# Attention and a rational MLP on one core: the last 64 keys added to the sum tiles by accumulating transfers, and early weights parked every fourth pair

## The chip, the cores and the metric

One Trainium2 chip, one of its cores. The time is the device time of the kernel in microseconds; the median of three runs before is 660.2 us (659.58 to 661.03).

## What is computed

Softmax attention with a soft cap on the scores, for 4 batches of 12 heads with 448 positions and 64 channels, and behind it an MLP with a rational activation on the 1792 x 768 result. All data are float32.

```python
scores = scale * np.matmul(q, k.transpose(0, 1, 3, 2))        # scale = 1 / 8
scores = cap * np.tanh(scores / cap)
scores = scores - np.max(scores, axis=-1, keepdims=True)
attn = np.exp(scores)
attn = attn / (np.sum(attn, axis=-1, keepdims=True) + 1e-09)
x = np.matmul(attn, v)                                        # then (4*448, 12*64)
h = x @ w_in                                                  # 768 -> 2048
P = a[0] + a[1] * h + a[2] * h**2 + a[3] * h**3
Q = 1.0 + np.abs(b[0]) * np.abs(h) + np.abs(b[1]) * h**2
out = (P / (Q + 1e-6)) @ w_out                                # 2048 -> 768
```

The cap bounds the scores, so for a small enough cap the kernel leaves out the maximum (its "bounded" branch, the one that runs here) and puts a scaled guard in place of the 1e-9.

## The kernel before

**Pairs.** The attention stage works on 24 pairs of heads; `p` counts them, two pairs make a group of four heads that is loaded at once, `ring_of` names the buffer. For a pair, `prep_k` and `prep_q` transpose K and Q on TensorE (L343 to L366) and VectorE splits them into a high and a low part (L350 to L384). `scores` (L429) multiplies a tile of 128 keys by all queries of both heads, three products of high and low parts; a pair has three such tiles (n = 0, 1, 2). The 64 keys that are left over, the tail, are done for two pairs together as tile n = 3, in the odd pair: its rows 0 to 63 belong to the even pair, 64 to 127 to the odd one. `softmax` runs Tanh (L440) and Exp (L457) on ScalarE. `pv` (L511) multiplies by V for the three full tiles, `pv_tails` (L528) adds the tails of both pairs, and VectorE copies the results into the tiles U (L535).

**Sums.** VectorE adds the three exponential tiles of a pair to a sum tile `es[p % 6]` (L463, twice per pair); the tail is not in it. `norm4(k)` (L580) sums over the keys by matmuls with columns of ones (L594), for four pairs at once, into the bank `mi`: eight products of the sum tiles and four of the tails, each two instructions, 24 in all. VectorE copies the result (L598), four small transfers on POOL gather it, VectorE adds the guard and takes the reciprocal (L605, L606), one transfer writes it to DRAM (`dn`), and four broadcast it to all partitions (`bc`). `xout` (L627) multiplies U by it, `split_x` (L638, L639) splits the result for the MLP. `norm4` is called in pairs 5, 9, 13, 17 and 21, each time for the four pairs that began five pairs before; `norm` (L538) does two pairs, in pair 23 and at the end, with 16 instructions (L556).

**Order.** `visits(p)` writes the order of the steps of a pair by hand. In an even pair: s0 s1 s2, transposes of pair p + 2, `pv` and the tails of pair p - 1. In an odd one: s0 s1 s2, the scores of tile 3, the sum if it is due, the softmax of tile 3, the transposes of pair p + 2, `pv` of p - 1. All of TensorE's work in this stage writes the key "turn" and so keeps the written order. The other engines get their order from `Plan.flush`: it runs through all work once with assumed costs, and takes on each engine the ready piece with the lowest number, less its `early`. Each engine then executes that order as it stands; POOL and SP issue the transfers in it.

**Early weights.** The weights arrive as 64 bit words. `load_w` fetches a block of 768 KB, `make_w` builds float32 from it (ScalarE L789; VectorE L791, L794, L797) in a scratch tile XA, which lies over the tiles U of pairs 15 and 16. Four blocks are loaded in pairs 3, 5, 7 and 9 and built in the pair after. The first two are split at once into a high and a low part (L820, L822); the last two are parked: written to DRAM (`w32`) and read back by `unpark` later.

**MLP.** `stage1` multiplies x by a block of w_in, 36 matmuls per unit (units 0 to 3: L858, in turns of 512 and 384 columns; later ones: L843, all of 512 ahead of all of 384), `rational` (L889 to L902) the activation, `stage2` (L928) multiplies by w_out, and the evictions (L955, L961) collect the sums.

Of the kernel before, what the change touches and what calls it, by code (L numbers as in the profile page):

```python
# [16 lines left out]
ALU = mybir.AluOpType  # L17
# [7 lines left out]
NES = 6  # L25
# [22 lines left out]
FILL = (4, 4)  # L48
# [4 lines left out]
EARLY_STEP = 2  # L53
# [5 lines left out]
SC_NS = 615  # L59
TURN_NS = 200  # L60
SHAPE_NS = 130
PV_NS = 2220
TAIL_NS = 870
D_NS = 1430
D4_NS = 2210
# [7 lines left out]
class Plan:  # L73
# [7 lines left out]
    def __init__(self):  # L81
        self.ops = []
        self.wr, self.rd = {}, {}
        self.n = 0
        self.free = [4500.0, 4600.0, 3700.0, 3700.0, 9900.0]
        self.dma_free = 11000.0
        self.where, self.over = {}, {}
# [94 lines left out]
def ring_of(g):  # L182

    return g % 2 if g else 2
# [63 lines left out]
class Body:  # L248
# [11 lines left out]
    def __init__(self, tc, io, cst, bounded):  # L260
# [16 lines left out]
        self.plan = Plan()  # L277
        self.loaded = {(0, 0), ("v32", 0), ("v", 0)}
        self.units = [(g, m, y) for g in range(self.NG) for m in range(self.B // 2) for y in range(self.NCH)]
        self.wn = 0  # L280

# [50 lines left out]
    def prep_k(self, p):  # L332
# [16 lines left out]
        self.op(PE, 440 + SHAPE_NS, tk, self.raw_keys(p, "rk"), [bk, "turn"], early=E_TR)  # L349
# [4 lines left out]
    def prep_q(self, p):  # L354
# [19 lines left out]
        self.op(PE, 390, tq, self.raw_keys(p, "rq"), [bq, "turn"], early=E_TR)  # L374
# [26 lines left out]
    def fill(self, n):  # L401

        z = self.io["arena_r"][:, 0:512]
        for _ in range(n):
            self.op(PE, 213, lambda: self.nc.tensor.matmul(self.PS[0][:, 1], z[:, 0:128], z, start=True, stop=True),
                    [], [("ps", 0), ("psb", 0), "turn"])
# [8 lines left out]
    def scores(self, p, n):  # L415
# [15 lines left out]
        first = n == 0 or p % 2 and n == 2  # L431
        self.op(PE, SC_NS * len(sets) + TURN_NS * first, run, [k for name, _ in sets for k in K(name)], w, early=E_SC)

    def softmax(self, p, n):
# [6 lines left out]
        if self.bounded:  # L441
            self.exp(p, n, e, [ek], e, ek)

    def etile(self, p, n):
# [4 lines left out]
        return self.e[ie], ("e", ie)  # L449

    def exp(self, p, n, src, sk, e, ek):
# [11 lines left out]
        self.op(DVE, dve_ns(896), lambda: nc.vector.tensor_tensor(es, a, e, ALU.add), [ek] + [ak] * (n == 1), ks)  # L463
# [33 lines left out]
    def pv(self, p):  # L497
# [16 lines left out]

        self.op(PE, PV_NS + SHAPE_NS, run, [("rv", ring_of(g), 0)] + [t[1] for t in tiles], [pk, "turn"])

    def pv_tails(self, p):
# [14 lines left out]
        self.op(PE, TAIL_NS, run, [("v32", ring_of(g), 0), ("v32", ring_of(g), 1), ek], ["pv", "mi", "turn"])  # L532
# [5 lines left out]
    def norm(self, k):  # L538
# [10 lines left out]

        def sums():  # L550
            for last in range(2):
                for j in range(2):
                    for x in range(2):
                        h = 32 * (2 * j + x)
                        st, mv = (self.half[x], tail[:, j]) if last else (self.ones, es[x][:, j])
                        m = nc.tensor.matmul(D[h:h + 32], st, mv, start=not last, stop=last == 1)  # L556
            return m

        self.op(PE, D_NS + SHAPE_NS, sums, [("es", (2 * k + x) % NES) for x in range(2)] + [tk, "ones"], [dk, "turn"])
# [20 lines left out]
    def norm4(self, k):  # L580
# [4 lines left out]
        tails = [self.etile(2 * (k + y), 3) for y in range(2)]  # L585
        es = [("es", (2 * k + x) % NES) for x in range(4)]

        def sums():
            for last in range(3):
                for y in range(2):  # L590
                    for j in range(2):
                        h = 32 * (2 * y + j)
                        st, mv = (self.both, tails[y][0]) if last == 2 else (self.unit[last], self.es[es[2 * y + last][1]])
                        m = nc.tensor.matmul(D[h:h + 32], st, mv[:, j], start=not last, stop=last == 2)  # L594
            return m

        self.op(PE, D4_NS + SHAPE_NS, sums, [*es, *(t[1] for t in tails), "ones"], [dk, "turn"])
# [43 lines left out]
    def attention(self):  # L641
# [33 lines left out]
        def visits(p):  # L675
# [10 lines left out]
            if p == 0:  # L686
                return [s0, s1, (k, 1), (q, 1), s2, (self.fill, FILL[0])]
            if p == 1:
                return [s0, (self.fill, FILL[1]), s1, (k, 2), s2, t, (q, 2), (k, 3), (q, 3), (pv, 0)]
            if not p % 2:  # L690
                return [s0, s1, s2, *new, (pv, p - 1), (tails, p - 1)]
            sums = (norm, p // 2 - 1)
            if p == P1 - 1:
                return [s0, s1, (pv, p - 1), sums, s2, t]
            four = [(norm4, p // 2 - 2)] * (p % 4 == 1)
            return [s0, s1, s2, (self.scores, p, 3), *four, (self.softmax, p, 3), *new, (pv, p - 1)]
# [637 lines left out]
```

## Time and profile before

| | us |
|---|---|
| median of three runs | 660.2 (659.58 to 661.03) |
| the profiled execution, its own time | 659.91 |
| its span, from the first to the last instruction | 657.9 |
| TensorE matmul busy (share of the span) | 647.8 (98%) |
| VectorE busy | 541.9 (82%) |
| ScalarE busy | 442.2 (67%) |
| POOL busy | 85.0 (13%) |

A row of the timeline begins with the start and the duration in microseconds, then the engine, the line of the kernel, the operation, target and sources, the count; in brackets stands the idle time before it and what ended it. Matmuls overlap, so the distance of two starts tells what a block took. In the table by stretches each engine has its busy time and, in brackets, its instructions; the granted clock is a share of full speed, and the DMA share is the mean over the core's 16 DMA engines. The attention stage ends at some 186 us, where the tails and the last sum are done.

### The profile page before, as it was taken

The numbers are of one execution on the slowest core, as the hardware profiler recorded it, in microseconds if no ns is written. First come the engines' busy times: TensorE is split into PE (matmuls) and PEld (weight loads), VectorE is DVE, ScalarE is ACT, GpSimd is POOL, SyncE is SP. The second block draws the span as 40 slices with busy tenths as digits, with TensorE's granted clock in tenths as the row PEclk, the third lists the DMA queues.
The fourth block names the chain that finished last, engine by engine and source line by source line (L and its number), as shares of the span: only waits on it lengthen the run. The fifth ranks groups of instructions, "written<-read, shape, count | busy, mean of one in ns | idle before, by whom it ended". The sixth has DMA issues, their size and how long they took to land.

```text
span 657.9 us, 9767 instructions
## 1 busy us (share of the span) xinstructions
PE 647.8 (98%) x3820; PEld 542.0 (82%) x3820; DVE 541.9 (82%) x662; ACT 442.2 (67%) x531; POOL 85.0 (13%) x141
## 2 busy tenths in 40 slices
PE   8999999999999999999999999999999999999996
PEld 5555555655478899999999999999999999999996
DVE  4789899899679987977987897899699789969653
ACT  5899999999857867875457466646646565663560
POOL 4013222321200000020012002101200210120030
PEclk9999999999999999999999999999999999999999
DMA  7757864943230332195158118614821671481086
GB/s 170 186 138 171 203 163 100 199 119 85 59 86 22 128 141 92 51 197 113 48 106 158 49 49 152 158 43 86 166 68 49 128 142 60 95 170 33 1 139 203
DMA packets 79095, 74.45 MB, mean 113 GB/s; under 512 B 48456, under 2 KB 67264, under 8 KB 79040
## 3 DMA queue, kind: packets, MB, share of 16 engines
q1 hardware_dynamic: 68240, 48.68, 25.7%
q0 software_dynamic: 9648, 24.80, 22.5%
q8 instruction: 32, 0.52, 0.3%
q10 hardware_dynamic: 1152, 0.25, 0.2%
q14 instruction: 23, 0.19, 0.1%
HBM read 47.98 MB, written 25.65 MB: 112 GB/s over the span
## 4 chain that ended last, share of the span: by engine, by line
PE 82%; DVE 6%; ACT 4%; DMA 3%; issue 3%; POOL 0%; SPq 0%; DVEq 0%; POOLq 0%; ACTq 0%
PE ps L843 31%; PE ps L928 17%; PE mi L928 9%; PE pv L928 9%; PE ps L429 6%; PE mi L511 3%; DMA arena_r<-dn 2%; ACT etiles L440 2%; PE mi L594 1%; PE pv L511 1%; ACT etiles L457 1%; PE pv L528 1%; PE ps L343 1%; DMA dn<-arena_f 1%; PE ps L366 1%
## 5 line engine op out<-in xcount | busy, mean ns | idle before, releaser
L843 PE MATMUL ps<-arena_r,ring 128*128 128x512 f32 (+1 forms) x924 | 207.6, 363 | 0.0
L843 PEld LDWEIGHTS ps<-arena_r,ring 128*128 128x128 f32 x924 | 167.7, 188 | 17.5
L295 POOL DMA_DIRECT2D out_dram<-arena_f x49 | 42.0, 863 | 423.6 <-ACT arena_f L955 423.6
L928 PE MATMUL ps<-arena_r,etiles 128*128 128x384 f32 x462 | 89.7, 335 | 0.6 <-ACT arena_f L955 0.5
L457 ACT ACTIVATE etiles<-etiles,acap 128x896 f32<-128x896 f32 x84 | 85.5, 1053 | 0.2
L440 ACT ACTIVATE etiles<-ps 128x896 f32<-128x896 f32 x84 | 74.7, 921 | 13.9 <-PE ps L429 13.7
L928 PEld LDWEIGHTS ps<-arena_r,etiles 128*128 128x128 f32 x462 | 80.8, 188 | 1.3 <-ACT arena_f L955 0.8
L928 PE MATMUL mi<-arena_r,etiles 128*128 128x384 f32 x231 | 77.2, 336 | 0.0
L928 PE MATMUL pv<-arena_r,etiles 128*128 128x384 f32 x231 | 77.0, 335 | 0.0
L429 PEld LDWEIGHTS ps<-arena_r 64*128 64x128 f32 x576 | 51.0, 184 | 25.2 <-ACT etiles L457 7.8
L889 ACT ACTIVATE arena_f<-ps,b 128x896 f32<-128x896 f32 x32 | 32.3, 1009 | 54.8 <-PE ps L843 54.7
L429 PE MATMUL ps<-arena_r 64*128 64x448 f32 x576 | 67.7, 376 | 1.2 <-DVE arena_r L384 0.9
L789 ACT ACTIVATE arena_f<-arena_f 128x768 f32<-128x768 f32 x32 | 29.4, 918 | 44.1 <-DMA arena_f<-in_moe_w_out_dram 31.0
L901 ACT CAST etiles<-arena_f 128x896 fp32r<-128x896 f32 x32 | 30.3, 946 | 42.0 <-DVE arena_f L900 42.0
L893 DVE SCALAR_TENSOR_TENSOR arena_f<-arena_f,bab 128x896 f32<-128x896 f32 x32 | 36.8, 1150 | 23.8 <-ACT arena_f L890 23.8
L898 DVE SCALAR_TENSOR_TENSOR arena_f<-arena_f,one 128x896 f32<-128x896 f32 x32 | 36.7, 1148 | 11.3 <-ACT arena_f L896 11.3
L928 PEld LDWEIGHTS pv<-arena_r,etiles 128*128 128x128 f32 x231 | 43.3, 188 | 0.6
L928 PEld LDWEIGHTS mi<-arena_r,etiles 128*128 128x128 f32 x231 | 43.3, 188 | 0.6
L928 PE MATMUL ps<-ring,etiles 128*128 128x384 f32 x210 | 42.0, 334 | 0.0
L902 DVE TENSOR_TENSOR etiles<-arena_f,etiles 128x896 fp32r<-128x896 f32 x32 | 34.9, 1089 | 7.0 <-ACT etiles L901 6.8
L891 ACT ACTIVATE arena_f<-ps,a 128x896 f32<-128x896 f32 x32 | 35.3, 1104 | 3.5 <-DVE arena_f L899 3.5
L897 DVE SCALAR_TENSOR_TENSOR arena_f<-arena_f,a,ps 128x896 f32<-128x896 f32 x32 | 36.6, 1144 | 0.4
(145 smaller groups left out, 1124.2 us busy)
## 6 DMA issues: line engine op xcount, KB each, us to landing
out_dram<-arena_f POOLq DMA_DIRECT2D x49, 384.0 KB, 6.2
arena_f<-in_moe_w_out_dram SPq DMA_DIRECT2D x16, 768.0 KB, 4.3
arena_f<-in_moe_w_in_dram SPq DMA_DIRECT2D x16, 768.0 KB, 4.8
out_dram<-arena_f SPq DMA_DIRECT2D x13, 384.0 KB, 2.5
ring<-in_q_dram SPq DMA_DIRECT2D x44, 112.0 KB, 3.6
arena_r<-dn POOLq DMA_DIRECT2D x20, 224.0 KB, 5.3
ring<-in_k_dram SPq DMA_DIRECT2D x33, 128.0 KB, 3.1
ring<-in_v_dram SPq DMA_DIRECT2D x11, 384.0 KB, 3.7
```

Of the source, the lines that this page charges most:

```text
L295: self.op(eng, (625 if local else 450) if eng == SP else 1050, lambda: e.dma_start(out, in_, **accum), r, w, nbytes=nbytes, **kw)
L429: m = nc.tensor.matmul(self.PS[i][:, j, 0:448], st[r], mv[r], start=y == 0, stop=y == len(ops) - 1)
L440: self.op(ACT, act_ns(896, True), lambda: nc.scalar.activation(e, ps, AF.Tanh), pk + ["table"], [ek], early=E_TANH)
L457: self.op(ACT, act_ns(size, sk[0][0] == "ps", 1), lambda: nc.scalar.activation(e, src, AF.Exp, scale=acap), sk + ["table"], [ek])
L843: r = nc.tensor.matmul(po[:, ts], w[:, y, kc], mv, start=kc == 0 and z == 0, stop=kc == KC - 1 and z == 2)
L889: self.op(ACT, act_ns(n, True, 1), lambda: T.activation(Bt, h, AF.Abs, scale=b[:, 0:1]), hk, bk)
L891: self.op(ACT, act_ns(n, True, 2), lambda: T.activation(A, h, AF.Identity, scale=a[:, 3:4], bias=a[:, 2:3]), hk, ak)
L893: self.op(DVE, dve_ns(n, 1), lambda: stt(Bt, C, bab[:, 1:2], Bt, ALU.mult, ALU.add), ck + ["bab"], bk)
L897: self.op(DVE, dve_ns(n, 1), lambda: stt(A, A, a[:, 1:2], h, ALU.add, ALU.mult), hk, ak)
L898: self.op(DVE, dve_ns(n, 1), lambda: stt(Bt, Bt, one, C, ALU.add, ALU.mult), ck, bk)
L902: self.op(DVE, dve_ns(n), lambda: V.tensor_tensor(GL(), A, f32(GH()), ALU.subtract), ak + K("gh", ig), K("gl", ig))
L928: r = nc.tensor.matmul(po[n][:, 0:384], st, mv[:, 384 * n:384 * n + 384], start=(y == 0 and x == 0), stop=(y == self.NCH - 1 and x == 2))
```

## The change

An accumulating transfer on POOL adds the two halves of a tail tile to the sum tiles of the two pairs (`add_tails`), for odd pairs from 5 to 21, once the exponentials of tile 3 and VectorE's adds of tile 2 are written. `norm4` leaves the tails out from its second call on, and `norm` in pair 23; the first `norm4` and the last `norm` keep them. The order is written as text; in pairs 9, 13 and 17 the sum (sums4) moves behind `pv`, the rest stands as before. VectorE's second add gets a higher priority in pairs 7, 11 and 15. `EARLY_STEP` goes from 2 to 4: the blocks are loaded in pairs 3, 7, 11 and 15 and built in 4, 8, 12 and 16. In units 0 to 3, `stage1` runs the three products of 512 columns ahead of the three of 384, for each of the six slices. The plan's assumed costs change by some per cent.

```diff
+ORDER = {
+    0: "s0 s1 k:1 q:1 s2 fill:4",
+    1: "s0 fill:4 s1 k:1 s2 t q:1 k:2 q:2 pv:-1",
+    "even": "s0 s1 s2 k:2 q:2 pv:-1 tails:-1",
+    "odd": "s0 s1 s2 score3 sums4 tanh3 k:2 q:2 pv:-1",
+    9: "s0 s1 s2 score3 tanh3 k:2 q:2 pv:-1 sums4",
+    13: "s0 s1 s2 score3 tanh3 k:2 q:2 pv:-1 sums4",
+    17: "s0 s1 s2 score3 tanh3 k:2 q:2 pv:-1 sums4",
+    -1: "s0 s1 pv:-1 sums s2 t",
+}
...
-EARLY_STEP = 2
+EARLY_STEP = 4
...
+ADDED = 4
...
         if self.bounded:
             self.exp(p, n, e, [ek], e, ek)
+        if self.bounded and n > 1 and p % 2:
+            self.add_tails(p, "s2" if n == 2 else "t")
...
+    def add_tails(self, p, part):
+
+        nc = self.nc
+        self.parts.add((p, part))
+        if p < ADDED or p == self.B * self.NP - 1 or not {(p, "s2"), (p, "t")} <= self.parts:
+            return
+        e, ek = self.etile(p, 3)
+        for x in range(2):
+            r, t = p - 1 + x, slice(64 * x, 64 * x + 64)
+            o, a = self.es[r % NES][t], e[t]
+            self.dma(POOL, o, a, [ek], [("es", r % NES)], accum_op=ALU.add)
...
-        self.op(DVE, dve_ns(896), lambda: nc.vector.tensor_tensor(es, a, e, ALU.add), [ek] + [ak] * (n == 1), ks)
+        self.op(DVE, dve_ns(896), lambda: nc.vector.tensor_tensor(es, a, e, ALU.add), [ek] + [ak] * (n == 1), ks,
+                early=E_PR * (n == 2 and p % 4 == 3 and ADDED < p < 16))
...
+        whole = self.bounded and not end
+
         def sums():
-            for last in range(2):
+            for last in range(1 if whole else 2):
...
-        tails = [self.etile(2 * (k + y), 3) for y in range(2)]
         es = [("es", (2 * k + x) % NES) for x in range(4)]
+        tails = [self.etile(2 * (k + y), 3) for y in range(2 * (2 * k < ADDED))]
+        end = 2 if tails else 1
 
         def sums():
-            for last in range(3):
+            for last in range(end + 1):
...
-                for z, (y, mv) in enumerate(((0, h), (0, lo), (1, h))):
-                    for ts, x in zip(parts, mv):
-                        r = nc.tensor.matmul(po[:, ts], w[:, y, kc], x,
+                for ts, *x in zip(parts, h, lo, h):
+                    for z, y in enumerate((0, 0, 1)):
+                        r = nc.tensor.matmul(po[:, ts], w[:, y, kc], x[z],
                                              start=kc == 0 and z == 0, stop=kc == KC - 1 and z == 2)
```

## Rows read from the trace of the kernel before

**Rows 1.** Busy time by stretches, one round of four pairs each: PE, PEld, DVE, ACT, POOL.
```profile
50.78:80.48 29.70, 28.68 (x218) 16.05 (x216) 26.77 (x40) 27.52 (x32) 6.47 (x13) 1.00 0.80 193
80.48:109.02 28.54, 28.47 (x218) 16.07 (x216) 27.22 (x42) 26.03 (x31) 8.64 (x15) 1.00 0.60 147
109.02:137.61 28.59, 28.52 (x218) 16.02 (x216) 25.91 (x38) 27.20 (x32) 5.41 (x10) 1.00 0.68 141
137.61:166.66 29.05, 28.73 (x218) 15.97 (x216) 27.87 (x41) 26.12 (x30) 8.74 (x17) 1.00 0.39 101
```

**Rows 2.** Waits of PE up to 240 us: total us, times, longest.
```profile
PE ps L343 <- ACT etiles L440: 0.8, 1, 0.8
```

**Rows 3.** Timeline of PE around the sum in pair 13.
```profile
103.25 0.57 PE L594 MATMUL mi<-arena_f 128*32 128x448 f32 x2
...
104.78 0.94 PE L594 MATMUL mi<-etiles,arena_f 128*32 128x448 f32 x8
105.64 0.55 PE L343 MATMUL ps<-ident,ring 128*128 128x128 f32 x3
...
109.02 1.28 PE L429 MATMUL ps<-arena_r 64*128 64x448 f32 x10
```

**Rows 4.** Timeline of PE at the sums in pairs 21 and 23.
```profile
160.89 0.57 PE L594 MATMUL mi<-extra,arena_f 128*32 128x448 f32 x2
...
175.83 0.96 PE L556 MATMUL mi<-arena_f 128*32 128x448 f32 x8
176.60 0.94 PE L556 MATMUL mi<-etiles,arena_f 128*32 128x448 f32 x8
177.47 2.09 PE L429 MATMUL ps<-arena_r 64*128 64x448 f32 x18
```

**Rows 5.** Timeline of PE in units 0 to 3 of the MLP and behind.
```profile
185.86 18.03 PE L858 MATMUL ps<-arena_r,ring 128*128 128x512 f32 x86
203.73 0.57 PE L858 MATMUL ps<-extra,ring 128*128 128x512 f32 x2
...
219.73 2.38 PE L928 MATMUL ps<-arena_r,etiles 128*128 128x384 f32 x12 [0.53 <-ACT arena_f L955]
```

**Rows 6.** The chain that ended last: start us, us, what.
```profile
186.61 5.14 DMA arena_r<-dn
...
222.11 4.12 PE ps L843 x18
...
230.41 3.12 PE ps L843 x18
```

**Rows 7.** The page's costliest groups: accumulating transfers issued by POOL.
```profile
L295 POOL DMA_DIRECT2D out_dram<-arena_f x49 | 42.0, 863 | 423.6 <-ACT arena_f L955 423.6
```

**Rows 8.** Timeline of DVE: the second add of pairs 11, 19 and 21.
```profile
99.19 1.08 DVE L463 TENSOR_TENSOR extra<-extra,etiles 128x896 f32<-128x896 f32 x1
...
153.29 1.09 DVE L463 TENSOR_TENSOR arena_f<-arena_f,etiles 128x896 f32<-128x896 f32 x1
...
166.85 1.08 DVE L463 TENSOR_TENSOR arena_f<-arena_f,etiles 128x896 f32<-128x896 f32 x1
```

**Rows 9.** Timeline of POOL: four broadcasts, issued back to back, in two rounds.
```profile
62.57 2.08 POOL L295 DMA_DIRECT2D arena_r<-dn  x4 [3.20 <-DMA dn<-arena_f]
...
119.81 2.08 POOL L295 DMA_DIRECT2D arena_r<-dn  x4 [2.25 <-DMA dn<-arena_f]
```

**Rows 10.** Timeline of DVE: multiplies that waited for a broadcast.
```profile
68.62 0.62 DVE L627 TENSOR_TENSOR arena_f<-arena_r,arena_f 128x448 f32<-128x448 f32 x1 [2.72 <-DMA arena_r<-dn]
...
126.72 0.62 DVE L627 TENSOR_TENSOR arena_f<-arena_r,arena_f 128x448 f32<-128x448 f32 x1 [2.25 <-DMA arena_r<-dn]
```

**Rows 11.** DMA issues: count, KB each, median us from issue to landing.
```profile
out_dram<-arena_f POOLq DMA_DIRECT2D x49, 384.0 KB, 6.2
...
w<-arena_f SPq DMA_DIRECT2D x2, 384.0 KB, 4.5
```

**Rows 12.** Groups by line and shape: one of VectorE's steps for a block.
```profile
L794 DVE SCALAR_TENSOR_TENSOR arena_f<-arena_f 128x768 int32<-128x768 int32 x32 | 30.5, 953 | 0.3
```

More of the change, by code (lines that the diff above doesn't have):

```diff
@@ L58 @@
 E_TANH = 6
[L59 to L65, printed above, removed]
+SC_NS = 621
+SHAPE_NS = 165
+PV_NS = 2240
+TAIL_NS = 746
+D_NS = 1493
+D4_NS = 2240
+ADDED = 4
 E_W = 10
@@ L430, in run @@
             return m
-        first = n == 0 or p % 2 and n == 2
-        self.op(PE, SC_NS * len(sets) + TURN_NS * first, run, [k for name, _ in sets for k in K(name)], w, early=E_SC)
+        self.op(PE, SC_NS * len(sets) + self.turn("s"), run, [k for name, _ in sets for k in K(name)], w, early=E_SC)
     def softmax(self, p, n):
@@ L513, in run @@
             return m
-        self.op(PE, PV_NS + SHAPE_NS, run, [("rv", ring_of(g), 0)] + [t[1] for t in tiles], [pk, "turn"])
+        self.op(PE, PV_NS + self.turn("pv"), run, [("rv", ring_of(g), 0)] + [t[1] for t in tiles], [pk, "turn"])
     def pv_tails(self, p):
@@ L530, in run @@
             return m
[L532 removed]
+        self.op(PE, TAIL_NS + self.turn("tails"), run, [("v32", ring_of(g), 0), ("v32", ring_of(g), 1), ek], ["pv", "mi", "turn"])
         for x in range(2):
@@ L555, in sums @@
                         st, mv = (self.half[x], tail[:, j]) if last else (self.ones, es[x][:, j])
-                        m = nc.tensor.matmul(D[h:h + 32], st, mv, start=not last, stop=last == 1)
+                        m = nc.tensor.matmul(D[h:h + 32], st, mv, start=not last, stop=last == 1 or whole)
             return m
-        self.op(PE, D_NS + SHAPE_NS, sums, [("es", (2 * k + x) % NES) for x in range(2)] + [tk, "ones"], [dk, "turn"])
+        self.op(PE, (D_NS // 2 if whole else D_NS) + self.turn("sums"), sums,
+                [("es", (2 * k + x) % NES) for x in range(2)] + [tk] * (not whole) + ["ones"], [dk, "turn"])
         self.op(DVE, dve_ns(448), lambda: nc.vector.tensor_copy(DB, D), [dk], ["db"], early=E_EV)
@@ L593, in sums @@
                         st, mv = (self.both, tails[y][0]) if last == 2 else (self.unit[last], self.es[es[2 * y + last][1]])
-                        m = nc.tensor.matmul(D[h:h + 32], st, mv[:, j], start=not last, stop=last == 2)
+                        m = nc.tensor.matmul(D[h:h + 32], st, mv[:, j], start=not last, stop=last == end)
             return m
-        self.op(PE, D4_NS + SHAPE_NS, sums, [*es, *(t[1] for t in tails), "ones"], [dk, "turn"])
+        self.op(PE, (D4_NS if tails else D_NS) + self.turn("sums"), sums, [*es, *(t[1] for t in tails), "ones"], [dk, "turn"])
         self.op(DVE, dve_ns(448), lambda: nc.vector.tensor_copy(DB, D), [dk], ["db"], early=E_EV)
@@ L685, in visits @@
                         (tails, p), (norm, p // 2)]
[L686 to L696, printed above, removed]
+            text = ORDER.get(p if p in ORDER else p - P1) or ORDER["odd" if p % 2 else "even"]
+            out = []
+            for w in text.split():
+                name, _, d = w.partition(":")
+                d = int(d or 0)
+                if name in ("k", "q") and p + d >= P1 or name == "sums4" and p % 4 != 1:
+                    continue
+                out.append(dict(s0=s0, s1=s1, s2=s2, t=t, k=(k, p + d), q=(q, p + d), pv=(pv, p + d), tails=(tails, p + d),
+                                sums=(norm, p // 2 - 1), score3=(self.scores, p, 3), tanh3=(self.softmax, p, 3),
+                                sums4=(norm4, p // 2 - 2), fill=(self.fill, d))[name])
+            return out
         for p in range(P1):
```

17 lines of the change are left out of this document (11 added, 6 removed).

## The prediction

> **What bounds the kernel now.** I read the four stretches between the sums first [rows 1], then what TensorE waits for [rows 2], then its order of work around a sum [rows 3, 4], then the queues that the new transfers join. Each stretch of rows 1 is one round of four pairs, about 28.5 to 29.7 us. TensorE is busy for all but 0.07 us of the second and third; the quickest round, 28.54 us, is therefore its own work. The granted clock is 1.00 in all four, the upper level, 2.4 GHz. The other engines are close behind: VectorE has 26.77 + 27.22 + 25.91 + 27.87 = 107.77 us of work in 29.70 + 28.54 + 28.59 + 29.05 = 115.88 us, ScalarE 106.87. Beyond the quickest round the others lose 1.16, 0.05 and 0.51 us, 1.7 us together; 0.8 us of it is one wait of TensorE for ScalarE [rows 2]. So the attention stage is bound by TensorE, with two engines that come next at once. Behind it, at 186 to 220 us, the chain runs through the last normalizations and VectorE, and from 219.73 us the MLP is TensorE without a gap [rows 5, 6].
>
> **Tail sums off TensorE.** A sum over four pairs starts at 103.25, its last third (the tails) at 104.78, and the transposes behind it at 105.64 [rows 3]. The tails cost 105.64 - 104.78 = 0.86 us, the other two thirds 1.53; since the change of shape into the transposes remains, I take what the same eight instructions cost between two like ones, 176.60 - 175.83 = 0.77 us [rows 4]. Of five such sums the one in pair 5 keeps its tails; those in pairs 9, 13, 17 and 21 lose them: 4 x 0.77 = **3.08 us**, all on TensorE. The sum of two pairs in pair 23 loses half of its 16 instructions, again 0.77 us. There the chain goes on through the third score tile, ScalarE and VectorE to the transfers at 186.61 [rows 6], and engines in between work in order, so I give it half, **0.4 us** (bounds 0 and 0.77).
>
> **The transfers that replace them.** Pairs 5, 7, ... 21 issue two each, 18 in all, 64 partitions x 896 words = 224 KB, on POOL. An accumulating one of 384 KB took 863 ns to issue [rows 7]; 18 x 0.86 = 15.5 us of POOL, which is busy 29.3 of 115.9 us [rows 1], so the issue is covered. If that cover were gone, what stands behind them in POOL's order would suffer: the tail rows of V for the next group, and the normalizing chain (four gathers, one write to DRAM, four broadcasts). Each pair of transfers waits for its exponential of the tail and for VectorE's second add, and holds POOL meanwhile.
>
> The new wait is that of the sum for the transfers. Its slack can be read: in pair 19 VectorE's second add ends at 153.29 + 1.09 = 154.38 [rows 8], and the sum in pair 21, which is not moved, starts at 160.89 [rows 4]: 6.5 us. In pair 11 the add ends at 100.27; the sum in pair 13 starts at 103.25, and the change moves it behind 3.38 us of other work (below), to 106.63: 6.4 us. For that pair the change lets the add go earlier as well. In pair 21 the add ends at 167.94 and the sum in pair 23 starts at 175.83: 7.9 us. The trace has no accumulating transfer within SBUF. Nearest are two plain ones of 224 KB, each to half of the partitions, issued back to back: from 62.57 and 119.81 [rows 9] to the multiply that waited for them at 68.62 and 126.72 [rows 10], 6.05 and 6.91 us with both issues in it. An accumulating one of 384 KB to DRAM landed in 6.2 us [rows 11]. So two need 6 to 7 us, up to 0.6 us more than the slack in pairs 11 and 19: 0 to 1.2 us of TensorE for both, and I take **+0.3 us**. DMA is at a share of 0.39 around pair 19, the least of the four stretches [rows 1], which speaks for the lower end; that accumulation reads its target first, for the upper.
>
> One rule of the Trainium skill speaks against this form of transfer. The rows show two half-height transfers landing 6.05 and 6.91 us after the first issue. By the Trainium skill ("SBUF — State Buffer", "Can I just issue two DMAs to hit both halves?") a transfer to partitions 0 to 63 and one to 64 to 127 do not add up their ports but run one behind the other. By that rule the sum would be that of the third rival below.
>
> **The moved sums.** In pairs 9, 13 and 17 the sum goes from before the transposes to behind the product with V. That distance is 109.02 - 105.64 = 3.38 us [rows 3]. On TensorE it costs nothing: as many changes of shape, and the score tile's ScalarE work gets the time instead. But everything that the sum releases goes with it: VectorE's copy, four gathers on POOL, reciprocal, write, four broadcasts, and the multiplies by the reciprocals. VectorE has stood still for those broadcasts for 2.72 and 2.25 us in the traced run [rows 10]. The plan in the code moves the multiplies back by what it expects, which includes the 3.38 us; it does not expect queueing behind the new transfers. I cost the move itself at 0, with 0 to +3 us as bounds: VectorE's work and these two stalls are 107.77 + 4.97 = 112.74 us, and the shortened rounds are 115.88 - 3.08 = 112.80 us long. A longer stall there has no cover left, except that four or five splits of 1 us can slide behind the last pair. The second cover is the bank: the copy now has only two score tiles and the transposes before the next product with V needs it, some 3 us where it had over 6.
>
> **Parked weights every fourth pair.** Work is not removed but spread: each block has three VectorE steps, two of them 0.95 us [rows 12], so about 2 us, one or two on ScalarE, a load, and for two of the four a write and a read back on SP. The first stretch (29.70 us) carried the second and the third block; it will carry one, which frees some 2 us on VectorE in the round with the largest loss. The last block moves to pair 16, where the scratch it is made in lies over the target of pair 15's result: that VectorE copy now waits for the park to land (4.5 us [rows 11]). If the block is made late this stops VectorE for up to 2 us, once; its bank is not wanted before the moved sum in pair 17, so I cost it at 0 to 0.5 us. Of the 1.7 us lost to waits I take back 0.4 (bounds -1 and 1.7): VectorE's margin of 0.06 us leaves no room for more. With 0.2 for the park, **-0.4 + 0.2 us**.
>
> **Stage 1's new order.** In units 0 to 3 of the MLP, matmuls of 512 and 384 columns alternate; 86 take 203.73 - 185.86 = 17.87 us, 207.8 ns each [rows 5]. Sorted ones take 4.12 and 3.12 us per 18, 201.1 ns on average [rows 6]. The change sorts them by three: two changes of width per six instead of six, so 144 x 6.7 ns x 2/3 = 0.64 us. TensorE then waits until 219.73 for ScalarE's eviction, 0.53 us of idle time [rows 5], behind VectorE's rational functions. It would only wait longer: **0**, at most 0.64.
>
> **Sum.** 659.91 us is the profiled execution's own time (span 657.9). 659.91 - 3.08 - 0.4 + 0.3 - 0.4 + 0.2 = 656.5. The median shown is 660.2, 0.3 above it; so **656.8**.
>
> **Rivals.**
> (1) All waits of the attention are recovered, with pair 23 and stage 1 in full: 660.2 - 3.08 - 0.77 - 1.7 - 0.64 = 654.0. For it: the largest loss is in the round that is relieved. Against: VectorE's margin. Chance 0.11, from 653.3 to 655.2.
> (2) VectorE and ScalarE are the next bound and take back most of the 3.08 us: the stalls for the broadcasts grow by about 1 us in each of the three moved rounds, and the 0.4 us of waits are not recovered: 656.8 + 3 x 1 + 0.4 = 660.2. For it: 112.74 against 112.80 us. Against: the splits can slide to where VectorE stands still. Chance 0.16, from 658.4 to 661.3. This is also the case in which the change doesn't do what it says: 40 instructions leave TensorE, and it waits as long.
> (3) The other side: the two transfers run one behind the other, each at its own 6 us, so 0.86 + 2 x 6.05 = 13 us from add to landing. Then TensorE stands still before the sums in pairs 13 and 21 for 13 - 6.4 and 13 - 6.5 us: 656.8 + 6.6 + 6.5 = 669.9, without what pairs 9 and 23 may add. It decides from a landing of 6.5 + 3.4 / 2 = 8.2 us on, where two such waits take the gain of 3.4 us. The two broadcasts that landed in 6 to 7 us speak against it; that none of them accumulates into SBUF leaves it possible. Chance 0.13, from 661.5 to 672. The rule of the skill cited above is this rival; by the rows so far, it does not hold in full.
>
> **How the numbers follow.** Forecast 0.60, with 655.2 to 658.4 around 656.8. Range: from 653.8, which leaves out a quarter of rival 1 (0.03), to 661.0, which takes in nearly all of rival 2 and leaves out rival 3 and the rest (0.15). A measurement of this kernel can tell 0.2%, 1.3 us, from no change: faster is below 658.9, slower above 661.5. Faster: 0.60 + 0.11 + 0.05 of rival 2 = 0.76; same, the rest of rival 2, 0.11; slower 0.13.
>
> **What would show it.** In the trace after: sums of 16 instructions in pairs 9 to 21, rounds of about 27.8 us between them, no idle time of TensorE before the sum in pairs 21 and 23 (rival 3 if there is, ended by a DMA), the waits of the multiplies for their broadcasts at 2 to 3 us each (rival 2 if much more), a span of units 0 to 3 shorter by 0.6 us with a longer wait at its end, and the MLP behind it unchanged. The prediction is wrong in its main term if the rounds are not shorter by 0.7 us with TensorE still without a gap.

## The result and the profile after

The changed kernel takes 662.88 us in the median (659.0 to 666.2), the kernel before 659.84 beside it: a ratio of 1.0052, 95% interval 1.0035 to 1.0068. It is slower by half a per cent, where 656.8 was forecast. Timed again with the experiments it took 664.27 (659.86 to 666.5), ratio 1.0062, 1.0043 to 1.0082.

The profiled execution of after, 659.0 us (span 657.1), is the shortest one of its eight; so its trace shows where time goes, not all of how much. First what TensorE waits for up to 240 us, as in [rows 2]: us in total, times, longest.

```profile
PE mi L629 <- DVE arena_f L566: 1.8, 1, 1.8
...
PE ps L446 <- DVE arena_r L400: 1.0, 2, 0.6
...
PE ps L446 <- ACT etiles L456: 0.5, 1, 0.5
...
PE mi L629 <- DMA extra<-etiles: 0.2, 1, 0.2
```

The lines have moved: scores L446, sums of four pairs L629, copies of the result out of its banks L566, steps of a block L824 to L832. The first line is new, and it is a term of the prediction. Around it, in the timelines of PE, DVE, SP's queue and DVE again:

```profile
137.55 1.71 PE L629 MATMUL mi<-arena_f 128*32 128x448 f32 x16 [1.80 <-DVE arena_f L566]
...
129.03 0.62 DVE L566 COPY arena_f<-pv 128x448 f32<-128x448 f32 x1
...
130.09 0.95 DVE L832 SCALAR_TENSOR_TENSOR arena_f<-arena_f 128x768 int32<-128x768 int32 x1
...
132.03 0.58 SPq L311 DMA_DIRECT2D w<-arena_f  x1
...
136.88 0.61 DVE L566 COPY arena_f<-mi 128x448 f32<-128x448 f32 x1
```

VectorE copies the first half of the result at 129.03. The second half, out of bank `mi`, comes 7.85 us later: its target lies under the scratch of the last block, whose write to DRAM is issued at 132.03 and has landed at 136.38. The sum in pair 17, now behind the product with V, needs that bank from 135.75 on, 6.72 us after the first half's copy, and waits 1.80 us.

The sums themselves are as short as forecast, 16 instructions (the x16 above; [rows 3] have the 24), and those of pairs 21 and 23 wait for nothing (against [rows 4]). That of pair 13 does wait for a transfer. Its bracket has 0.21 us, the time in which TensorE did nothing; but from its first instruction to the scores behind it are 108.88 - 106.10 = 2.78 us, where the same 16 instructions take 139.19 - 137.55 = 1.64 in pair 17, and as long in pair 9. So the wait costs 1.14 us. Of the fence below, the first three lines are POOL's timeline: a transfer of pair 9 that held POOL for 9.94 us; the broadcasts, which waited 4.90 us for the write to DRAM where [rows 9] have 3.20 and 2.25; and the transfers of pair 11 behind them. The fourth is the chain of waits (start us, us, what) with their landing, the last four are PE's timeline at the sums in pairs 13 and 17.

```profile
82.27 0.87 POOL L311 DMA_DIRECT2D arena_f<-etiles  x1 [9.94 <-ACT etiles L456]
...
96.24 2.05 POOL L311 DMA_DIRECT2D arena_r<-dn  x4 [4.90 <-DMA dn<-arena_f]
98.27 1.74 POOL L311 DMA_DIRECT2D extra<-etiles  x2
...
98.81 9.14 DMA extra<-etiles
...
106.10 0.57 PE L629 MATMUL mi<-arena_f 128*32 128x448 f32 x2
...
108.00 0.94 PE L629 MATMUL mi<-extra,arena_f 128*32 128x448 f32 x4 [0.21 <-DMA extra<-etiles]
108.88 2.09 PE L446 MATMUL ps<-arena_r 64*128 64x448 f32 x18
...
139.19 2.12 PE L446 MATMUL ps<-arena_r 64*128 64x448 f32 x18
```

Busy time by stretches, in the columns of [rows 1] but from the product with V of pair 5 to that of pair 9, and so on to pair 21:

```profile
54.17:82.83 28.66, 27.99 (x210) 15.78 (x209) 24.41 (x37) 26.08 (x31) 7.85 (x13) 1.00 0.91 188
82.83:111.87 29.04, 28.77 (x209) 15.93 (x209) 26.68 (x40) 25.60 (x30) 12.96 (x21) 1.00 1.03 204
111.87:142.21 30.34, 28.00 (x209) 15.80 (x208) 29.30 (x43) 29.66 (x35) 11.48 (x18) 1.00 0.86 180
142.21:169.06 26.85, 26.78 (x202) 14.96 (x201) 26.06 (x38) 24.62 (x29) 11.00 (x18) 1.00 0.76 156
```

The column before the last matters: the DMA engines' share (a sum over packets, which can pass 1) is 0.91, 1.03, 0.86 and 0.76, where the rounds of [rows 1] have 0.80, 0.60, 0.68 and 0.39. On the same marks the rounds of before are 29.70, 28.54, 29.12 and 27.55 us long: the first and the last are shorter now, the second, with the wait in pair 13, and the third, with the wait in pair 17, longer. TensorE has gaps of 0.67, 0.27, 2.34 and 0.07 us.

Behind the attention little has changed. Six more of stage 1's matmuls stand ahead of the last product with V, which begins at 181.83 for 180.90; TensorE then waits 0.56 us for ScalarE's eviction, where [rows 5] have 0.53, goes on at 219.16 for 219.73, and needs 437.95 us from there to the end, for 438.22.

```profile
219.16 2.35 PE L963 MATMUL ps<-arena_r,etiles 128*128 128x384 f32 x12 [0.56 <-ACT arena_f L990]
```

### The profile page after: what moved, and what is told of

Read it like the earlier page. It is cut to its first block, busy times and chain, and to the rows that moved or that the text cites. A ratio compares the mean times of both kernels' runs of the same rounds, so it can differ in the third digit from the quotient of the medians.

```text
span 657.1 us, 9741 instructions
## 1 busy us (share of the span) xinstructions
PE 645.2 (98%) x3780; PEld 541.4 (82%) x3780; DVE 541.7 (82%) x662; ACT 441.4 (67%) x531; POOL 101.4 (15%) x159
## 4 chain that ended last, share of the span: by engine, by line
PE 70%; DMA 14%; DVE 7%; issue 4%; ACT 3%; POOL 2%; SPq 0%; DVEq 0%; ACTq 0%; POOLq 0%
PE ps L878 31%; PE ps L963 17%; PE mi L963 9%; PE pv L963 9%; DMA a<-in_moe_a_dram 7%; DMA dn<-arena_f 2%; DMA arena_f<-arena_f 2%; DMA arena_r<-dn 2%; PE ps L446 1%; DMA extra<-etiles 1%; POOL arena_f L311 1%; ACT etiles L487 1%; ACT etiles L456 1%; PE mi L542 1%; DVE arena_f L662 1%
## 5 line engine op out<-in xcount | busy, mean ns | idle before, releaser
L446 PEld LDWEIGHTS ps<-arena_r 64*128 64x128 f32 x576 | 51.0, 184 | 25.9 <-ACT etiles L456 7.3
L446 PE MATMUL ps<-arena_r 64*128 64x448 f32 x576 | 67.8, 376 | 1.8 <-DVE arena_r L400 1.0
L824 ACT ACTIVATE arena_f<-arena_f 128x768 f32<-128x768 f32 x32 | 29.4, 918 | 38.7 <-DMA arena_f<-in_moe_w_out_dram 27.5
L963 PEld LDWEIGHTS ps<-ring,etiles 128*128 128x128 f32 x210 | 36.9, 188 | 0.0
```

What stands on the lines that cost most here:

```text
L446: m = nc.tensor.matmul(self.PS[i][:, j, 0:448], st[r], mv[r], start=y == 0, stop=y == len(ops) - 1)
L963: r = nc.tensor.matmul(po[n][:, 0:384], st, mv[:, 384 * n:384 * n + 384], start=(y == 0 and x == 0), stop=(y == self.NCH - 1 and x == 2))
```

## The experiments

All times are medians; each ratio is to the kernel before, timed on the same chip (659.2 to 659.9 us).

| run | edit | us | ratio, 95% |
|---|---|---|---|
| e1_after | the change | 664.27 | 1.0062 (1.0043 to 1.0082) |
| e1_step2 | blocks every second pair | 659.44 | 1.0000 (0.9988 to 1.0012) |
| e1_noadd | no transfers, no moved sums | 673.30 | 1.0219 (1.0198 to 1.0241) |
| e1_chain_sp | normalizing chain on SP | 678.87 | 1.0290 (1.0255 to 1.0325) |
| e2_xa | last block in other scratch | 659.55 | 0.9997 (0.9986 to 1.0008) |
| e2_step3 | blocks every third pair | 659.90 | 1.0005 (0.9991 to 1.0018) |
| e2_noadd_step2 | no transfers or moves, every second pair | 660.20 | 1.0008 (0.9998 to 1.0018) |
| e3_both | that, and transfers on top | 663.98 | 1.0083 (1.0060 to 1.0106) |
| e3_nomove | transfers in place of the tails | 660.93 | 1.0023 (1.0011 to 1.0035) |
| e3_xa_at4 | e2_xa, blocks one pair later | 670.50 | 1.0166 (1.0134 to 1.0199) |
| e4_both_tiny | e3_both, 16 of 896 words | 659.63 | 1.0002 (0.9991 to 1.0012) |
| e4_step2_tiny | e1_step2, 16 of 896 words | 658.44 | 0.9977 (0.9963 to 0.9990) |
| e4_added8 | e1_step2, transfers from pair 9 on | 657.27 | 0.9960 (0.9949 to 0.9971) |
| e4_added12 | e1_step2, transfers from pair 13 on | 656.90 | 0.9961 (0.9948 to 0.9974) |
| e5_no9 | e1_step2, sum in pair 9 not moved | 659.01 | 0.9999 (0.9988 to 1.0010) |
| e5_xa_added8 | e2_xa, transfers from pair 9 on | 665.68 | 1.0094 (1.0081 to 1.0108) |

**1. Which part is it?**

```diff
 e1_step2:  -EARLY_STEP = 4       +EARLY_STEP = 2
 e1_noadd:  -ADDED = 4            +ADDED = 99         (orders 9, 13, 17 removed, whole = False)
```

> The changed kernel once more, for a trace of another execution: the traced one took 659.0 us, the median of eight is 662.9. Theory Q (POOL's queue: the accumulating transfers and the normalizing chain hold each other up in one in-order queue): 662 to 664 us, and the 4 us against the first trace lie in TensorE's waits before sums or for broadcasts. Theory P (the last block is parked late, pair 15's copy waits for it and the moved sum in pair 17 for the copy): they lie in the wait before the sum in pair 17, which took 1.8 us in the first trace. Theory C (clock): the attention is as long as in the first trace and a stretch shows the lower granted clock.

> The changed kernel with the four blocks of weights loaded and parked every second pair, as before the change. Theory P: 1.8 us or more come back, 658 to 661 us, no wait before the sum in pair 17. Theory Q: 662 to 664 us, or more, since the blocks now share the DMA engines with the first accumulating transfers.

> The changed kernel without the accumulating transfers: the tails stay in TensorE's sums, and so the sums stay where they were in pairs 9, 13 and 17. Parking, stage 1 and the plan's costs are those of the change. Theory Q: the kernel before, 659.5 to 660.5 us, or a little under it. Theory P: 662 us or more, with a wait around pair 17.

With the blocks every second pair again the kernel is level with the one before; every fourth pair costs 4.8 us (664.27 - 659.44; 4.1 by the ratios). Without the transfers they cost 13 us (673.30 against the 660.20 of e2_noadd_step2): the sum of four pairs still stands ahead of the transposes, so it wants the bank earlier. Its longest wait of TensorE and its stretches of 8 us (columns as in rows 1):

```profile
PE mi L626 <- DVE arena_f L563: 4.2, 1, 4.2
...
136.00:144.00 8.00, 3.84 (x34) 2.08 (x34) 7.97 (x11) 8.00 (x10) 0.43 (x1) 0.81 0.40 128
144.00:152.00 8.00, 8.00 (x52) 3.66 (x46) 5.52 (x9) 2.70 (x4) 2.29 (x4) 0.76 0.43 106
```

One wait of 4.2 us (four others, for VectorE and ScalarE, come to 5.7), and behind it TensorE runs at a granted clock of 0.81 and 0.76, between its levels of 2.4 and 1.2 GHz. That is the second price of a standstill.

**2. Is it the scratch, or the spreading?**

```diff
 e2_xa:     -  X, xk = self.XA, ("x", "A")
            +  n3 = (which, f) == EARLY[3]
            +  X, xk = (self.XA3, ("x", "A3")) if n3 else (self.XA, ("x", "A"))
            ...
            +  keys("W3", 4 * 2304, (("x", "A3"), self.DM))
            +  self.XA3 = io["arena_f"][:, 2304:2304 + self.DM]
 e2_step3:  -EARLY_STEP = 4       +EARLY_STEP = 3
```

> The changed kernel with one edit: the last of the four parked blocks, built in pair 16, uses 768 words of scratch above the first raw buffer's place (free by then) and not the scratch that lies over the target of pair 15's result. Nothing is left out. Theory P (the scratch over the target is what costs): VectorE copies pair 15's result without waiting for the park, the wait of the moved sum in pair 17 for that copy (1.7 to 1.8 us) is gone, the distance from the product of pair 15 to that of pair 17 falls from 17.2 to about 15 us, the granted clock stays at 1.00, and the median comes to 658.5 to 659.5, level with or a little below the kernel before. Rival (the place is not what costs: a block's work of VectorE and ScalarE in pair 16, or the later loads, do): the median stays at 662.5 to 664.5.

> The changed kernel with the four blocks every third pair (loaded in pairs 3, 6, 9, 12, built in 4, 7, 10, 13), so that the last is parked two pairs before pair 15's result is copied. Nothing is left out. Theory P: no wait of the sum in pair 17 for the copy, and as the blocks stand further apart than every second pair, fewer waits of TensorE for ScalarE in pairs 6 to 10: 658 to 659.5. Rival (spreading itself costs): 661 or more, between 659.4 for every second pair and 664.3 for every fourth.

Both are back at the time of before. With the scratch alone moved, VectorE's copy follows at once and the sum in pair 17 waits for nothing (timelines of DVE and PE):

```profile
130.47 0.62 DVE L566 COPY arena_f<-pv 128x448 f32<-128x448 f32 x1
131.00 0.61 DVE L566 COPY arena_f<-mi 128x448 f32<-128x448 f32 x1
...
137.12 1.71 PE L629 MATMUL mi<-arena_f 128*32 128x448 f32 x16
```

So the place of the scratch is shown to be the cause of the 4.7 us (664.27 - 659.55; 4.3 by the ratios), not the spreading. Only 1.8 us of that is the wait itself. The gain that was forecast does not come with it: e2_xa is no faster than the kernel before, and in its trace the sum in pair 13 takes 4.07 us for 1.64, since its transfers land late.

**3. Where do the other 2 to 3 us come from?** The changed kernel again, one profiled execution each.

> The changed kernel once more, one look, for the granted clock. Theory P with the clock: if the run is a long one (663 or more), the granted clock falls below 1.00 for some us behind the wait of the sum in pair 17 and nowhere else; if it is a short one (659 to 661), the clock is 1.00 throughout although the wait is there.

> The changed kernel again, one look, for the granted clock in an execution of 664 us or more, if this is one: below 1.00 for some us behind the wait of the sum in pair 17 and nowhere else. If it is a short one, the clock is 1.00 throughout.

The trace of e1_after, an execution of 660.91 us, has the wait of pair 17 as it was, 1.79 us. Its span is 2.0 us longer than the first one's; 1.15 of them lie in the round from pair 9 to pair 13 (30.19 us for 29.04), where the sum in pair 13 takes 3.18 us.

The two others took 662.10 and 662.63 us. In the second the wait was 1.97 us, and the clock fell behind it (timeline of PE, then stretches):

```profile
137.92 2.50 PE L629 MATMUL mi<-arena_f 128*32 128x448 f32 x16 [1.97 <-DVE arena_f L566]
140.35 2.89 PE L446 MATMUL ps<-arena_r 64*128 64x448 f32 x18
...
128.00:136.00 8.00, 6.99 (x54) 4.26 (x50) 7.73 (x11) 8.00 (x10) 1.48 (x3) 1.00 1.06 228
136.00:144.00 8.00, 6.08 (x42) 3.60 (x42) 6.44 (x9) 5.89 (x8) 4.01 (x6) 0.79 0.66 93
144.00:152.00 8.00, 8.00 (x63) 4.67 (x63) 7.21 (x12) 7.66 (x10) 1.77 (x3) 1.00 0.93 198
```

The sum took 2.50 us for 1.71, the scores behind it 2.89 for 2.09: 1.6 us more. In the three traces of this kernel with waits of 1.79, 1.80 and 1.81 us (e1_after, the profile after, e2_after_b) the clock stayed at 1.00. Of the twelve timed executions of e1_after, the six with a mean clock of 0.998 or more took 659.9 to 664.7 us, the six below 664.3 to 666.5. My numbers for where it falls (executions of 663 or 664 us and more) were off: one of 662.63 showed it. Whether every long execution has it is not shown; the clocks by execution only go that way.

**4. What is the accumulation worth?** e2_noadd_step2 has neither transfers nor moved sums; e3_both adds the transfers and keeps the tails on TensorE, so it counts the last 64 keys twice; e3_nomove takes the tails off; e1_step2 moves the sums.

```diff
 e3_both:   -whole = self.bounded and not end      +whole = False
            -for y in range(2 * (2 * k < ADDED))   +for y in range(2)
            (EARLY_STEP = 2, orders 9, 13, 17 removed)
```

> The changed kernel without the accumulating transfers and the moved sums (the last 64 keys are summed on TensorE again), blocks every second pair: of the change only stage 1's order and the plan's new costs are left. Theory P: 659.5 to 660.5, the same as the kernel before, which makes the accumulation alone worth 0 to 1 us, and blocks every fourth pair alone (673.3) worth -13. Rival (stage 1's order and the plan's costs take back what the accumulation gives): 661 to 662.5.

> Blocks every second pair, sums not moved, the accumulating transfers AND the tails on TensorE, so that the last 64 keys are counted twice: it prices the 18 transfers and the sums' wait for them, with no instruction taken off TensorE. Without the transfers this kernel took 660.2. Theory T (the transfers have a price that eats the gain: POOL's queue holds the normalizing chain, the DMA engines are near full): 661.5 to 663.5, with waits of the sums for the transfers and of TensorE for VectorE or ScalarE. Rival V (the transfers are free, and the gain is lost because TensorE isn't the bound): 660 to 660.8.

> The same without the tails on TensorE (40 instructions less, 3.1 us at 0.77 us for eight), sums still ahead of the transposes in pairs 9, 13 and 17. Theory T: 3 us less than with both, 658.5 to 660, since TensorE is the bound, but for waits of the sums for the transfers. Rival V: at most 1.5 us less than with both. Against the same kernel with the sums moved (659.4) it prices the moves: at 0 by the prediction, up to 1 us above it if the sums in pairs 13 and 17 now wait for the transfers.

By the ratios, times 659.8: stage 1's order and the plan's costs +0.5 us; the 18 transfers, with the sums not moved, +4.9 (plus or minus 1.7); the 40 instructions -4.0 (1.7); the moved sums -1.5 (1.1); the blocks every fourth pair +4.1 (1.5). Within its interval the step of the instructions agrees with the 3.5 us of the prediction. The transfers cost as much again. In the trace of e3_both the sum in pair 13 waits for them (timeline of PE):

```profile
104.81 0.57 PE L626 MATMUL mi<-arena_f 128*32 128x448 f32 x2
...
107.83 0.57 PE L626 MATMUL mi<-extra,arena_f 128*32 128x448 f32 x2 [1.33 <-DMA extra<-etiles]
...
109.46 0.55 PE L356 MATMUL ps<-ident,ring 128*128 128x128 f32 x3
```

It takes 4.65 us to the transposes, where the kernel without transfers takes 2.39 (104.67 to 107.06 us): 2.26 us, about half of the price.

**5. Their bytes, or their place in POOL's order?** Every transfer cut to 64 x 16 words, the orders of all engines the same, but for the size (e4_step2_tiny so leaves nearly all of the last 64 keys out of the sums):

```diff
+            o, a = o[:, 0, 0:16], a[:, 0, 0:16]
```

> The kernel with both the transfers and the tails on TensorE (663.98), every transfer cut to 16 of its 896 words per partition: 64 x 16 words, 4 KB for 224 KB, at the same places of POOL's order and with the same waits and the same orders of the engines; 16 of the 896 sums count the last 64 keys twice. It separates the transfers' bytes from their issue. Theory B (bytes: the DMA engines are near full at 80 to 136 us, so K, Q, V, the blocks and the broadcasts land later, and the transfers too): 660 to 661.5, near the 660.2 without transfers. Theory O (order: on POOL the transfers hold the gathers and broadcasts while they wait for ScalarE and VectorE): 663 to 664.5, as with the full transfers.

> The changed kernel with blocks every second pair (659.4), its transfers cut in the same way to 16 of 896 words, so that nearly all of the last 64 keys is left out of the sums: what the change would give if its transfers moved no bytes. Theory B: 656 to 657.5, which is the 3.1 to 3.5 us of the instructions taken off TensorE. Theory O: 658.5 to 659.5, no better than with the full transfers.

Without their bytes the transfers cost nothing: 663.98 becomes 659.63, and the order is the same. So, with the sums not moved, it is the bytes that cost. Three kernels from 96 to 112 us, without transfers, with them, with tiny ones (columns as in rows 1):

```profile
96.00:112.00 16.00, 15.94 (x128) 8.80 (x128) 15.64 (x24) 14.78 (x18) 3.47 (x6) 1.00 0.80 160
```

```profile
96.00:112.00 16.00, 14.38 (x108) 7.04 (x106) 13.15 (x20) 13.53 (x16) 4.44 (x7) 1.00 0.82 162
```

```profile
96.00:112.00 16.00, 16.00 (x124) 8.78 (x123) 14.95 (x22) 14.34 (x17) 6.21 (x10) 1.00 0.80 151
```

TensorE works 15.94, 14.38 and 16.00 of 16 us there, at a DMA share that hardly differs. What differs is the landing: the second transfer of pair 11, issued at 100.64 us, lands at 107.78 in e3_both; issued at 99.34 and tiny it lands at 104.51, and the sum in pair 13 takes 2.69 us. That is some 2 of the 4.4 us; where the rest goes isn't located. From 64 to 80 us the share goes from 0.82 to 1.08 with the transfers, and is 0.96 with tiny ones. The second expectation failed: with bytes gone, e4_step2_tiny gains 1.05 us on the kernel before (1.5 by the ratio) and 1.2 on e4_both_tiny, not 3. With the sums moved, then, the bytes cost less, 1.5 us (1.2) from e1_step2 to this. What takes the rest of the gain back is open; no run separates it. Its trace has a wait of 0.92 us of stage 1 for VectorE's split of x, at 206.13 us, that e4_both_tiny's does not have.

**6. Fewer transfers.**

```diff
 e4_added8:   -ADDED = 4   +ADDED = 8    (order 9 removed)
 e4_added12:  -ADDED = 4   +ADDED = 12   (orders 9 and 13 removed)
 e5_no9:      order 9 removed alone
```

> Blocks every second pair, transfers only from pair 9 on: the sum in pair 9 keeps its tails and its place ahead of the transposes, and the four transfers of pairs 5 and 7 are gone. Nothing is left out. Theory B: the sum in pair 9 costs 0.8 us again, and four transfers less at 50 to 90 us, beside the blocks' loads, give it back: 659 to 660. Theory O says the same of POOL's queue; the run shows whether each round pays for itself.

> The same with transfers only from pair 13 on, where the DMA engines were least busy before (share 0.39 at 138 to 167 us): the sums in pairs 9 and 13 keep their tails (1.5 us on TensorE). Nothing is left out. Theory B: the transfers cost next to nothing there, and the sums in pairs 17, 21 and 23 gain 1.5 to 2.3 us: 658 to 659, below the kernel before. Rival (each transfer costs the same wherever it stands): 659.5 to 660.2, no gain.

> Blocks every second pair, transfers from pair 5 on as in the change, but the sum in pair 9 stays ahead of the transposes. Leaving out the four transfers of pairs 5 and 7 together with this move, and giving the sum in pair 9 its tails back, made the kernel 2.2 us faster (659.4 to 657.3); this run has the move undone alone. Nothing is left out. Theory F (the four transfers cost it, beside the blocks' loads and the first rows of K, Q and V): 659 to 660.5. Rival M (the moved sum in pair 9 costs it): 656.5 to 657.5.

Both are faster than the kernel before, by 0.4%, 2.6 us: the two best kernels of this study. Undoing the move alone does nothing (659.01), so it is the four transfers of pairs 5 and 7 that cost 0.9999 - 0.9960, some 2.6 us, although the sum in pair 9 got its tails back (0.8 us by rows 4). `ADDED` = 8 also takes VectorE's add in pair 7 back to its old place; that was not tried alone. Nor are the bytes all that these four cost, as far as two intervals that overlap a little can tell: all 18 without their bytes gave less (e4_step2_tiny, 658.44). And the share of the DMA engines alone does not decide: it is 1.17 from 96 to 112 us in e4_added8, more than in e3_both. I had expected 659 to 660 of e4_added8. The transfers of pairs 9 and 11 pay for themselves, no more: the two kernels are level.

**7. Loads in step with the normalizing chain.** With blocks every fourth pair, a block's load of 768 KB is issued in pairs 7, 11 and 15, where the chain of the sums of pairs 5, 9 and 13 writes to DRAM and broadcasts.

```diff
 e3_xa_at4:    e2_xa with  -EARLY_AT = 3   +EARLY_AT = 4    (XA3 at word 3072)
 e5_xa_added8: e2_xa with  -ADDED = 4      +ADDED = 8       (order 9 removed)
```

> The changed kernel with the last block built in other scratch (so that pair 15's result is copied without waiting) and all four blocks one pair later (loaded in pairs 4, 8, 12, 16), so that a block's load of 768 KB is no longer issued just ahead of the small write to DRAM that the broadcasts wait for (in pairs 11 and 15 that write landed in 5.0 to 6.4 us with the load beside it, in 1.7 without). Nothing is left out. Theory L (the loads in step with the normalizing chain hold the broadcasts, and with them the transfers behind them on POOL): waits for the write of 1.4 to 2.5 us, no wait of the sum in pair 13 for the transfers (1.3 us with the scratch alone moved), 658 to 659. Rival (the load delays the broadcasts instead of the write, nothing is won): 659.5, as with the scratch alone moved.

> The changed kernel, blocks every fourth pair as it has them, with the two repairs: the last block built in other scratch, and transfers only from pair 9 on (the sum in pair 9 keeps its tails and its place). Nothing is left out. If the scratch and the early transfers are all that is wrong with the change: 656.5 to 657.8, level with the 657.3 of blocks every second pair, below the kernel before. Rival (loads in step with the normalizing chain cost as well, since the write before the broadcasts lands in 5 to 6 us beside them): 658.5 to 659.5.

Both are slower than anything expected of them. Of e5_xa_added8, the load in SP's queue, VectorE's wait, TensorE's, and a stretch:

```profile
90.70 0.43 SPq L310 DMA_DIRECT2D arena_f<-in_moe_w_in_dram  x1
...
103.19 1.16 DVE L661 TENSOR_TENSOR arena_f<-arena_r,arena_f 128x448 f32<-128x448 f32 x2 [4.27 <-DMA arena_r<-dn]
...
106.79 1.49 PE L445 MATMUL ps<-arena_r 64*128 64x448 f32 x6 [2.40 <-DVE arena_r L399]
109.57 2.61 PE L445 MATMUL ps<-arena_r 64*128 64x448 f32 x12 [1.30 <-ACT etiles L455]
...
104.00:112.00 8.00, 4.30 (x22) 2.65 (x20) 8.00 (x13) 4.31 (x7) 0.53 (x1) 0.65 0.72 132
```

VectorE waits 4.27 us in order for the broadcasts, the casts that the scores need stand behind that, TensorE waits 2.40, and the clock is 0.65 in that stretch. This is rival (2) of the prediction in kind. In e4_added8, with the same transfers and no block's load there, VectorE waits 1.87 us for these broadcasts and TensorE 0.77, at a clock of 1.00; that the load makes the difference is argued from this, not tried alone. In e3_xa_at4 the load of pair 12 was issued at 90.87 us, 0.86 ahead of the same write, which landed after 6.08: a pair later by the program is not later by the clock. That kernel also waited 2.66 us for a transfer in the sum of pair 21.

**8. The chain on another queue.** Gathers, write and broadcasts of the four-pair sums issued by SP, so that POOL's transfers don't hold them.

```diff
-            self.dma(POOL, sc[16 * h:16 * h + 16], ...
+            self.dma(SP, sc[16 * h:16 * h + 16], ...
...                                  (the write to dn and the broadcasts likewise)
```

> The changed kernel with the normalizing chain of the four-pair sums (gathers, write to DRAM, broadcasts) issued on SP; POOL keeps the accumulating transfers and the tail rows of V. Theory Q: transfers land 4 to 6 us after the add, no wait of TensorE for a transfer, 656 to 659 us. Theory P: unchanged, 662 to 664 us. If the transfers themselves are slow, by a landing of 9 us as in the first trace, TensorE still waits before the sums in pairs 13 and 21.

678.87 us: TensorE waits 6.3 us for ScalarE's and 7.4 us for VectorE's results, the longest 3.2. SP works in order: it stands up to 7.5 us for the copy of the sums and 6.0 for the write, and behind these waits stand the loads of K, Q and the blocks. So this repair costs 14.6 us more.

## Why the prediction was wrong

**Tails off TensorE: right.** 3.08 us and 0.4 were forecast for the 40 instructions; e3_both and e3_nomove differ by 3.05 us in the medians, 4.0 (1.7) by the ratios. That the first figure is so close is luck: their waits differ as well.

**The transfers: the step that failed first.** I priced them as one wait of the sums, +0.3 us between 0 and 1.2, with POOL's issue covered. With the sums not moved they cost 4.9 us, and nothing when cut to 16 words; with the sums moved their bytes cost 1.5 (1.2), and without those of pairs 5 and 7 the kernel is 2.6 us faster. The wait that I named is there: in the four traces of the changed kernel the sum in pair 13 loses 0.73 to 1.74 us, that in pair 21 nothing. What I had wrong is the time to the landing, 6 to 7 us for two from [rows 9, 10]. In pair 11 VectorE's add ends at 96.01 us, but POOL issues the two at 98.27, behind the write and the broadcasts of the sum that was itself moved, and they land at 107.95: 11.9 us after the add. I had read the DMA share of the rounds [rows 1] only for the landing of the transfers themselves, and not for what 4 MB more do to the rest. The waits that the traces show do not make up the whole of it; how the four transfers of pairs 5 and 7 cost 2.6 us stays open.

**The park: the step that failed at the end.** I named the right wait, VectorE's copy of pair 15 for the park, and gave it 0 to 0.5 us because the bank "is not wanted before the moved sum in pair 17". That is where it was wanted: the sum needed it 6.72 us after the first half's copy, and the second half's copy, behind the park, came after 7.85. It cost 1.8 us in the trace and 4.7 in the medians. The +0.2 of the sum was mis-sized by that.

**The clock: not in the sum.** I counted waits at their length. In six of the traces here a wait of TensorE of 1.77 us or more was followed by a stretch below 1.00; in e3_after_c that costs 1.6 us on top of 1.97.

**The moved sums**: 0 was forecast, with bounds to the slower side; e3_nomove to e1_step2 gives -1.5 us (1.1). In the traces it is the sums' wait for the transfers: unmoved, those of pairs 9 and 13 take 2.67 and 1.95 us, moved 1.64 each, 1.3 us in all. **Stage 1's order**: 0 forecast; alone with the plan's costs +0.5 (-0.1 to 1.2 by its interval), no gain, as said.

**The rivals.** (2) was nearest in kind for the kernel as changed: the gain is taken back beside TensorE. But its sign, longer stalls of VectorE for the broadcasts, is not in the profile after, which has one of 2.48 us where [rows 10] have two; in the runs it is the transfers' bytes and the park. (3), two transfers one behind the other, is not what happened: issued 0.54 us apart behind nothing else but broadcasts, at 126.35 and 126.89 us, they landed after 5.51 and 7.47 us, so 2.5 us apart and not 6. Yet its point of decision, 8.2 us from add to landing, was passed in pair 11, for another reason: they stood behind the broadcasts. The rule of the Trainium skill ("SBUF — State Buffer", "Can I just issue two DMAs to hit both halves?") holds in that the second half lands behind the first; the price of it here was 2.5 us, and such a transfer alone took 4.2 to 4.5. The Trainium skill says in "DMA: Bandwidth & Descriptors" ("Issuing engines are not separate DMA queues") that transfers of all queues run on the same 16 engines and interleave; the traces agree: the write that POOL issues for the broadcasts landed in 5.0 to 6.4 us with SP's load of a block issued 0.86 to 2.7 us before it, and in 1.70 at best without.

Of the marks set for the trace, the shorter sums, pairs 21 and 23 without a wait, and the MLP unchanged came out; rounds of about 27.8 us, and the longer wait behind units 0 to 3, did not.

## What to carry to other kernels

Before moving work from a bound engine to DMA, ask behind what each transfer will stand in its queue and what its bytes delay, and price the time from the last write of its sources to its landing; here 18 transfers of 224 KB took back all that they gave, and leaving out the first four made the same change pay. When a step is moved in time, list every buffer that lies over its scratch and who next wants the bank behind it. A standstill of the matrix engine of some 2 us can cost more than its length; look at the granted clock behind it.

## What the runs showed of the hardware

- An accumulating transfer within SBUF, 64 partitions x 896 words, lands 4.2 to 4.5 us after its issue with little else under way, and 5 to 10 us behind four broadcasts or beside loads. One of 64 x 16 words takes 1.9 to 2.1 us alone, but up to 7.9 behind broadcasts (e4_both_tiny): there what is ahead of it sets the time, not its size.
- The chain's write of 14 KB to DRAM landed in 1.70 us at best, mostly in 2 to 4, and in 5.0 to 6.4 us where a block's load of 768 KB had been issued 0.86 to 2.7 us before. With the load 0.3 to 0.4 us before it took 3.5 to 5.9; without one it came near once each in e5_no9 (4.97) and e5_xa_added8 (5.42).
- The granted clock in the stretch of 8 us around and behind a wait of TensorE: 0.87 with 1.77 us, 0.79 with 1.97, 0.60 with 2.02, 0.79 with 2.26, 0.65 with 2.40, 0.63 with 3.04, 0.90 with 3.15, 0.81 with 4.16; but 1.00 with 1.79 to 1.81, 1.91, 2.00, 2.66 and 3.00. The length of the wait alone doesn't settle it.
